# Keeping converted weights in a DRAM scratch: an attention and squared-ReLU MLP kernel on one core

## The chip, the core and the metric

The kernel runs on one core of a Trainium2 chip. The core has TensorE (PE; its weight loads are shown as PEld), VectorE (DVE), ScalarE (ACT), GpSimd (POOL) and SyncE (SP), which here only issues DMAs. Times are microseconds on the device for one execution.

## What is computed

q, k and v have the shape (4, 12, 448, 64): four batches, twelve heads. The weights are arrays of 64-bit floats, w_in 768 x 2048 and w_out 2048 x 768. The output is 1792 x 768 in 32-bit floats.

```python
scores = scale * np.matmul(q, k.transpose(0, 1, 3, 2))
scores = np.where(mask, -1000000000.0, scores)      # causal
attn = softmax(scores)
x = (attn @ v), heads side by side                  # 1792 x 768
h = np.maximum(x @ w_in, 0.0)
out = (h * h @ w_out).astype(np.float32)
```

## The kernel before

The tokens are worked in two halves of 896 (two batches each). The heads go in pairs: twelve pairs of the first half, then twelve of the second, whose results are stored to a DRAM tensor `x_dram` (line 435) and loaded back later (line 591). A pair takes scores on PE (line 327), the row maximum on DVE (line 340), the exponential on ACT (line 344), a scaling on POOL (line 353), transposes on PE (line 367) and the product with v (line 387).

The MLP runs in four groups of 512 of the 2048 inner columns, once for each half. A group has a first product, x by w_in (lines 490 to 492, `h_unit`), and a second one, the squares by w_out (lines 526 to 528, `o_unit`). Each number is kept as two parts, a high one rounded to PE's input format and a low one that holds the rest, and three matmuls make one product: high by high, high by low, low by high. Tiles with a 2 in front of their columns (`x`, `wi`, `g`, `wo`) hold both parts.

The weights come as 64-bit words. `piece` (line 441) brings one block: for w_in 128 x 512 (six blocks a group, tile `wi`), for w_out 128 x 384 (eight a group, tile `wo`). It loads the raw words (line 467, three buffers), has ACT make two intermediate words, has DVE shift, add and combine them into a 32-bit float (lines 475, 243 and 478), and splits that into the two parts (lines 250 and 247 on POOL, or line 240 on ACT and 243 on DVE). Each half does this for all 56 blocks.

The order of all instructions comes from a planner (class `Plan`). Every step gives an engine or a choice of engines with a duration, what it reads and writes, and a rank; the planner takes at each turn the step that can start first by its own clock, and the rank decides between equals. The emitted order of each engine is that of the planned starts. Nearly all DMAs are issued by SP in that order: q, k and v loads (lines 290 and 302), raw weights, x tiles and outputs. An issue that has to wait holds up all that stand behind it on SP. Buffers of the odd pairs (`b...`) are given up after the twelfth pair, and `wo` lies in their place (`swap`). In the first group of the first half, the first product is done for the first six pairs while later pairs are still in work.

Of the kernel before, what the change touches and what calls it, by code (L numbers as in the profile page):

```python
# [8 lines left out]
F32 = mybir.dt.float32  # L9
# [7 lines left out]
PE, ACT, DVE, POOL, DMA, DMA2 = range(6)  # L17
# [131 lines left out]
def kernel(  # L149
# [17 lines left out]
    nc = tc.nc  # L167
# [3 lines left out]
    P = 128  # L171
# [3 lines left out]
    NP = H // 2  # L175
# [3 lines left out]
    GF = 4  # L179
    NG = DFF // P // GF  # L180
    CH = DM // 2
# [23 lines left out]
    plan = Plan()  # L205
# [7 lines left out]
    wi_t = const.tile([P, 2, NP, GF * P], F32R, name="wi")  # L213
# [16 lines left out]
    for i in range(2):  # L230
        m = mask[i * QC:(i + 1) * QC, S - QC:]
        nc.gpsimd.affine_select(
            out=m, in_=m, pattern=[[-1, QC]], base=0,
# [203 lines left out]


    late = {"wo": None, "acc": None}

    def piece(rank, kind, gr, a, ch, after):
        if kind == "i":
# [121 lines left out]
    swap = [plan.op(0.0, [(DMA, 0.0, enter)], after=list(plan.ops))]  # L564

    def group(ph, gr, rank, step, begin):

        for c in range(NP):
            piece(begin + (rank - begin) * (c + 0.5) / NP, "i", gr, c, 0, ())
        begin = rank  # L570
        if ph == 0 and gr == 0:
            r = NP * PAIR + 16
            for f in range(GF):
                r = h_unit(f, 0, r, (start - r) / (GF - f) / NP)
            for f in range(GF):
                rank = h_unit(f, 1, rank, H_US * step)
        else:
            for f in range(GF):
                for h in range(2):
                    rank = h_unit(f, h, rank, H_US * step)  # L580
        for i in range(2 * GF):
            piece(begin + (rank - begin) * (i + 0.5) / 8, "o", gr, i % GF, i // GF, swap)
        begin = rank
        for ch in range(2):
            for t in range(NT):
                rank = o_unit(ph, gr, t, ch, rank, O_US * step, swap)
        return begin, rank
# [8 lines left out]
    rank, begin = start, 10.0  # L596
    rest = NG * (2 * GF * NP * H_US + 2 * NT * GF * O_US) - GF * NP * H_US
    for gr in range(NG):
        begin, rank = group(0, gr, rank, (rest + NA * 7.0) / rest, begin)
# [4 lines left out]
    for ph in range(1, NPH):  # L604
        for gr in range(NG):
            begin, rank = group(ph, gr, rank, 1.0, begin)
# [33 lines left out]
```

## Time and profile before

| | |
|---|---|
| timed runs | 642.58, 639.98, 642.56 us; median 642.56 |
| the profiled execution, first to last instruction | 638.4 us (no other time is given for it) |
| PE, PEld, DVE busy | 97%, 85%, 71% |
| ACT, POOL busy | 56%, 62% |
| DMA | 78.61 MB, mean 123 GB/s |
| HBM read, written | 69.60 MB, 8.26 MB |

Busy shares are of the span. The profile also has a row of the clock granted to TensorE by slices, the groups of instructions by source line with what ended the idle time before them, the waits, and the chain of waits: the work that ended last, followed back. In names, buffer numbers are left out: `raw<-in_moe_w_in_dram` is a load into any of the three raw buffers.

### The profile page before, as it was taken

The numbers are of one execution on the slowest core, as the hardware profiler recorded it, in microseconds if no ns is written. First come the engines' busy times: TensorE is split into PE (matmuls) and PEld (weight loads), VectorE is DVE, ScalarE is ACT, GpSimd is POOL, SyncE is SP. The second block draws the span as 40 slices with busy tenths as digits, with TensorE's granted clock in tenths as the row PEclk, the third lists the DMA queues.
The fourth block names the chain that finished last, engine by engine and source line by source line (L and its number), as shares of the span: only waits on it lengthen the run. The fifth ranks groups of instructions, "written<-read, shape, count | busy, mean of one in ns | idle before, by whom it ended". The sixth has DMA issues, their size and how long they took to land.

```text
span 638.4 us, 11482 instructions
## 1 busy us (share of the span) xinstructions
PE 619.2 (97%) x3936; PEld 544.8 (85%) x3936; DVE 450.4 (71%) x911; ACT 356.7 (56%) x856; POOL 395.8 (62%) x498
## 2 busy tenths in 40 slices
PE   3999999999999999999999999999999999999997
PEld 2666777798888898789888889999999999999997
DVE  5789865686668787678885479759845993897022
ACT  4789977676787456675557553545653344333300
POOL 1567854775678655767576688876657556656410
PEclk9799999999999999999999999999999999999999
DMA  9898931545574546544463258723541453141022
GB/s 156 158 201 150 186 80 31 109 154 152 118 173 130 151 98 155 152 96 115 126 159 100 77 164 248 210 73 109 158 130 34 108 155 101 59 123 50 1 87 87
DMA packets 134779, 78.61 MB, mean 123 GB/s; under 512 B 113729, under 2 KB 120385, under 8 KB 134721
## 3 DMA queue, kind: packets, MB, share of 16 engines
q1 hardware_dynamic: 131008, 77.42, 47.2%
q10 hardware_dynamic: 3712, 0.46, 0.5%
q8 instruction: 31, 0.51, 0.3%
q14 instruction: 28, 0.22, 0.1%
HBM read 69.60 MB, written 8.26 MB: 122 GB/s over the span
## 4 chain that ended last, share of the span: by engine, by line
PE 84%; DVE 5%; DMA 3%; POOL 3%; ACT 2%; issue 1%; SPq 0%; DVEq 0%; POOLq 0%; ACTq 0%
PE ps L526 12%; PE ps L527 12%; PE ps L528 12%; PE ps L490 11%; PE ps L491 11%; PE ps L492 11%; PE ps L387 6%; PE ps L367 5%; PE ps L327 4%; POOL ap L353 3%; DVE ps L340 2%; DMA v<-in_v_dram 1%; DMA bq<-in_q_dram 1%; ACT ap L344 1%; DMA aq<-in_q_dram 1%
## 5 line engine op out<-in xcount | busy, mean ns | idle before, releaser
L526 PE MATMUL ps<-wo,g 128*128 128x384 f32 x448 | 153.2, 342 | 0.0
L527 PE MATMUL ps<-wo,g 128*128 128x384 f32 x448 | 151.2, 338 | 0.0
L528 PE MATMUL ps<-wo,g 128*128 128x384 f32 x448 | 151.2, 337 | 0.0
L490 PE MATMUL ps<-x,wi 128*128 128x448 f32 x384 | 145.0, 378 | 0.6 <-ACT x L240 0.6
L491 PE MATMUL ps<-x,wi 128*128 128x448 f32 x384 | 140.6, 366 | 0.2 <-DVE x L243 0.2
L492 PE MATMUL ps<-x,wi 128*128 128x448 f32 x384 | 140.5, 366 | 0.0
L240 ACT ACTIVATE b<-raw 128x384 int32<-128x384 uint32 (+1 forms) x112 | 68.3, 610 | 89.1 <-DVE z L243 80.3
L243 DVE CUSTOM_DVE_ANT_0 z<-z,b 128x768 uint16<-128x768 uint16 (+1 forms) x112 | 102.9, 919 | 8.8 <-ACT b L240 1.9
L478 DVE SCALAR_TENSOR_TENSOR z<-raw,z 128x384 int32<-128x384 int32 (+1 forms) x112 | 94.8, 846 | 2.9
L353 POOL TENSOR_SCALAR ap<-ap,asm 128x448 f32<-128x448 f32 (+6 forms) x123 | 71.5, 600 | 35.1 <-DVE asm L411 21.8
L340 DVE CUSTOM_DVE_ANT_0 ps<-ps,mask 128x448 f32<-128x448 f32 (+6 forms) x168 | 68.8, 443 | 33.9 <-PE ps L327 24.9
L240 ACT ACTIVATE z<-raw 128x384 f32<-128x384 f32 (+1 forms) x112 | 67.8, 609 | 32.6 <-POOL wi L247 15.6
L526 PEld LDWEIGHTS ps<-wo,g 128*128 128x128 f32 x448 | 84.2, 188 | 1.4 <-issue 1.0
L527 PEld LDWEIGHTS ps<-wo,g 128*128 128x128 f32 x448 | 84.2, 188 | 0.1
L528 PEld LDWEIGHTS ps<-wo,g 128*128 128x128 f32 x448 | 84.1, 188 | 0.0
L490 PEld LDWEIGHTS ps<-x,wi 128*128 128x128 f32 x384 | 72.2, 188 | 9.0 <-issue 1.7
L475 DVE TENSOR_SCALAR z<-z 128x384 int32<-128x384 int32 (+1 forms) x112 | 63.3, 565 | 23.3 <-ACT z L240 23.0
L243 DVE TENSOR_TENSOR acc<-ps,acc 128x384 f32<-128x384 f32 x84 | 46.0, 550 | 46.1 <-PE ps L528 45.8
L492 PEld LDWEIGHTS ps<-x,wi 128*128 128x128 f32 x384 | 72.1, 188 | 6.1
L491 PEld LDWEIGHTS ps<-x,wi 128*128 128x128 f32 x384 | 72.2, 188 | 5.8 <-DVE x L243 0.5
L344 ACT ACTIVATE ap<-ps,mx 128x448 f32<-128x448 f32 (+6 forms) x126 | 58.7, 481 | 14.3 <-DVE mx L340 13.9
L247 POOL TENSOR_TENSOR g<-r,g 128x448 fp32r<-128x448 f32 x52 | 64.9, 1249 | 2.4
(65 smaller groups left out, 848.3 us busy)
## 6 DMA issues: line engine op xcount, KB each, us to landing
raw<-in_moe_w_in_dram SPq DMA_DIRECT2D x48, 512.0 KB, 3.9
raw<-in_moe_w_out_dram SPq DMA_DIRECT2D x64, 384.0 KB, 3.4
out_dram<-acc SPq DMA_DIRECT2D x28, 192.0 KB, 2.5
v<-in_v_dram SPq DMA_DIRECT2D x24, 192.0 KB, 4.0
ak<-in_k_dram SPq DMA_DIRECT2D x72, 56.0 KB, 2.7
aq<-in_q_dram SPq DMA_DIRECT2D x68, 56.0 KB, 2.6
x_dram<-xs SPq DMA_DIRECT2D x12, 224.0 KB, 3.8
xs<-x_dram SPq DMA_DIRECT2D x12, 224.0 KB, 2.7
```

The source lines that it names most:

```text
L240: return (ACT, t_act(n, psum, more), lambda: nc.scalar.activation(dst(), src(), func, **kw))
L243: return (DVE, t_dve(n) + more, lambda: nc.vector.tensor_tensor(out=dst(), in0=a(), in1=b(), op=op))
L340: plan.op(at, [(DVE, t_dve(w), lambda: nc.vector.tensor_tensor_reduce(out=at_(), in0=at_(), in1=mask[:, S - w:], scale=-SCALE, scalar=3.0e ...
L344: plan.op(at, [(ACT, t_act(w, True, 0.5), lambda: nc.scalar.activation(probabilities(c), at_(), AF.Exp, bias=mx.t, scale=-1.0, accum_out=s ...
L353: (POOL, 0.0005 * CW[c] + 0.34, lambda: nc.gpsimd.tensor_scalar(*operands(), 1.0, op0=ALU.mult, op1=ALU.mult)),
L478: plan.op(rank - 2, [(DVE, t_dve(n) + 0.2, lambda: nc.vector.scalar_tensor_tensor(out=z(), in0=word(1), scalar=-2 ** 31, in1=z(), op0=ALU. ...
L490: nc.tensor.matmul(o, w[:, 0], x[:, 0], start=c == 0, stop=False)
L491: nc.tensor.matmul(o, w[:, 0], x[:, 1], start=False, stop=False)
L492: nc.tensor.matmul(o, w[:, 1], x[:, 0], start=False, stop=c == NP - 1)
L526: nc.tensor.matmul(res(), g[:, 0], w[:, 0], start=f == 0, stop=False)
L527: nc.tensor.matmul(res(), g[:, 0], w[:, 1], start=False, stop=False)
L528: nc.tensor.matmul(res(), g[:, 1], w[:, 0], start=False, stop=f == GF - 1)
```

## The change

The scratch `w_dram` has a place for the two parts of every block, as 32-bit floats: 128 x 2 x 512 for w_in, 128 x 2 x 384 for w_out, 8 bytes a weight as in the raw form. In the first half (`ph == 0`) each block is converted as before and then stored from `wi` or `wo` into its place (`keep`, rank + 2). In the second half nothing is converted: `fetch` loads both parts straight into `wi` or `wo`. There is no buffer between, so a `fetch` is ordered behind the matmuls that read the old block. Each counts 1.7 us of the planner's DMA queue.

```diff
--- before.py
+++ after.py
@@ -437,6 +437,28 @@
 
 
     late = {"wo": None, "acc": None}
+    w_dram = {
+        "i": nc.dram_tensor("wi_split", (NG, NP, P, 2, GF * P), F32, kind="Internal").ap(),
+        "o": nc.dram_tensor("wo_split", (NG, 2 * GF, P, 2, CH), F32, kind="Internal").ap(),
+    }
+
+    def dst_of(kind, a, ch):
+        t = wi_t[:, :, a] if kind == "i" else late["wo"][:, :, a, ch * CH:(ch + 1) * CH]
+        return t.bitcast(F32)
+
+    def place_of(kind, gr, a, ch):
+        i = a if kind == "i" else a + GF * ch
+        return w_dram[kind][gr, i], ("wd", kind, gr, i), ("wi", a) if kind == "i" else ("wo", a, ch)
+
+    def keep(rank, kind, gr, a, ch):
+        place, saved, key = place_of(kind, gr, a, ch)
+        plan.op(rank, [(DMA, 1.7, lambda: nc.sync.dma_start(out=place, in_=dst_of(kind, a, ch)))],
+                [(key, 0), (key, 1)], [saved])
+
+    def fetch(rank, kind, gr, a, ch):
+        place, saved, key = place_of(kind, gr, a, ch)
+        plan.op(rank, [(DMA, 1.7, lambda: nc.sync.dma_start(out=dst_of(kind, a, ch), in_=place))],
+                [saved], [(key, 0), (key, 1)])
 
     def piece(rank, kind, gr, a, ch, after):
         if kind == "i":
@@ -565,8 +587,15 @@
 
     def group(ph, gr, rank, step, begin):
 
+        def weights(rank, *which):
+            if ph == 0:
+                piece(rank, *which, swap if which[0] == "o" else ())
+                keep(rank + 2, *which)
+            else:
+                fetch(rank, *which)
+
         for c in range(NP):
-            piece(begin + (rank - begin) * (c + 0.5) / NP, "i", gr, c, 0, ())
+            weights(begin + (rank - begin) * (c + 0.5) / NP, "i", gr, c, 0)
         begin = rank
         if ph == 0 and gr == 0:
             r = NP * PAIR + 16
@@ -579,7 +608,7 @@
                 for h in range(2):
                     rank = h_unit(f, h, rank, H_US * step)
         for i in range(2 * GF):
-            piece(begin + (rank - begin) * (i + 0.5) / 8, "o", gr, i % GF, i // GF, swap)
+            weights(begin + (rank - begin) * (i + 0.5) / 8, "o", gr, i % GF, i // GF)
         begin = rank
         for ch in range(2):
             for t in range(NT):
```

The queue of SP among the early heads, around the fifth to seventh pair: `ak` and `bk` are k loads of an odd and an even pair (the first pair is an `a`), `aq` and `bq` their q loads, `raw_80` to `raw_82` the three raw buffers, `v_90` one of two v buffers. Before:

```order
L467 DMA raw_81<-in_moe_w_in_dram 128x512
L290 DMA bk<-in_k_dram 32x14x32 x4
L290 DMA bq<-in_q_dram 32x14x32 x4
L290 DMA ak<-in_k_dram 32x14x32 x4
L290 DMA aq<-in_q_dram 32x14x32 x4
L467 DMA raw_82<-in_moe_w_in_dram 128x512
L467 DMA raw_80<-in_moe_w_in_dram 128x512
L467 DMA raw_81<-in_moe_w_in_dram 128x512
L302 DMA v_90<-in_v_dram 128x6x64 x3
L302 DMA v_90<-in_v_dram 64x6x64
```

Below is the same place in the changed kernel, where `wi_split` is the scratch for w_in:

```order
L489 DMA raw_81<-in_moe_w_in_dram 128x512
L290 DMA bk<-in_k_dram 32x14x32 x2
L455 DMA wi_split<-wi 256x1x512
L290 DMA bk<-in_k_dram 32x14x32 x2
L290 DMA bq<-in_q_dram 32x14x32 x4
L290 DMA ak<-in_k_dram 32x14x32 x4
L290 DMA aq<-in_q_dram 32x14x32 x4
L489 DMA raw_82<-in_moe_w_in_dram 128x512
L489 DMA raw_80<-in_moe_w_in_dram 128x512
L302 DMA v_90<-in_v_dram 128x6x64 x3
L302 DMA v_90<-in_v_dram 64x6x64
L455 DMA wi_split<-wi 256x1x512
```

A store stands between the second and third k load of the sixth pair, another behind the v loads, and one of the three raw loads ahead of the v loads has gone further back.

PE, around the eighth pair of heads (`b...` are its tiles, `a...` those of the pairs beside it): line 367 transposes, 327 scores, 387 the product with v, and 490 to 492 (after: 512 to 514) the first product, where `x_68` is the sixth tile of x, which goes with the sixth block of w_in. Before:

```order
L490 MATMUL ps_108<-x_68,wi 128x448
L491 MATMUL ps_108<-x_68,wi 128x448
L492 MATMUL ps_108<-x_68,wi 128x448
L490 MATMUL ps_105<-x_68,wi 128x448
L491 MATMUL ps_105<-x_68,wi 128x448
L492 MATMUL ps_105<-x_68,wi 128x448
L367 MATMUL ps_103<-ident,bp 128x128 x4
L490 MATMUL ps_104<-x_63,wi 128x448
L491 MATMUL ps_104<-x_63,wi 128x448
L492 MATMUL ps_104<-x_63,wi 128x448
L490 MATMUL ps_104<-x_64,wi 128x448
L491 MATMUL ps_104<-x_64,wi 128x448
```

In the changed kernel the first rows of PE with `x_68` have these around them:

```order
L387 MATMUL ps_109<-bpt,v_90 64x64 x2
L367 MATMUL ps_103<-ident,ap 128x128 x4
L367 MATMUL ps_104<-ident,ap 128x128 x4
L367 MATMUL ps_107<-ident,ap 128x128 x4
L367 MATMUL ps_103<-ident,ap 128x128 x4
L512 MATMUL ps_108<-x_68,wi 128x448
L513 MATMUL ps_108<-x_68,wi 128x448
L514 MATMUL ps_108<-x_68,wi 128x448
L512 MATMUL ps_105<-x_68,wi 128x448
L513 MATMUL ps_105<-x_68,wi 128x448
L514 MATMUL ps_105<-x_68,wi 128x448
L512 MATMUL ps_109<-x_63,wi 128x448
```

The matmuls with `x_68` stood ahead of the transposes of the eighth pair; now they stand behind that pair's whole work and the next pair's transposes.

SP around the start of the second half: `acc` is the output tile of the first half, `wo_split` the scratch for w_out. Before:

```order
L467 DMA raw_82<-in_moe_w_out_dram 128x384
L544 DMA out_dram<-acc 128x384 x2
L467 DMA raw_80<-in_moe_w_out_dram 128x384
L544 DMA out_dram<-acc 128x384
L467 DMA raw_81<-in_moe_w_in_dram 128x512
```

In the changed kernel the last outputs of the first half are followed by these:

```order
L566 DMA out_dram<-acc 128x384
L460 DMA wo<-wo_split 128x2x384
L566 DMA out_dram<-acc 128x384
L460 DMA wo<-wo_split 128x2x384 x2
L460 DMA wi<-wi_split 128x2x512 x6
L460 DMA wo<-wo_split 128x2x384 x8
```

Where raw loads stood, the loads of both parts stand in blocks of six and eight in the order of use.

## Rows read from the trace of the kernel before

**Rows 1.** The page: busy us, share and instructions of each engine.
```profile
PE 619.2 (97%) x3936; PEld 544.8 (85%) x3936; DVE 450.4 (71%) x911; ACT 356.7 (56%) x856; POOL 395.8 (62%) x498
```

**Rows 2.** Windows of 40 us: length, busy us of PE, PEld, DVE, ACT, POOL, clock, DMA, GB/s.
```profile
0.00:20.00 20.00, 9.51 (x68) 5.54 (x69) 11.94 (x48) 9.87 (x33) 5.51 (x18) 0.86 0.91 156
...
340.00:380.00 40.00, 38.95 (x242) 33.32 (x241) 22.18 (x41) 22.45 (x53) 30.43 (x36) 1.00 0.35 106
380.00:420.00 40.00, 40.00 (x213) 38.53 (x212) 35.01 (x48) 19.69 (x36) 30.28 (x32) 1.00 0.71 206
...
620.00:638.40 18.40, 14.84 (x86) 14.51 (x84) 4.46 (x8) 0.00 (x0) 0.00 (x0) 1.00 0.26 91
```

**Rows 3.** Windows by stage: the early heads, the rest of the first half, the second half.
```profile
30.00:78.60 48.60, 46.49 (x407) 31.33 (x407) 43.25 (x139) 44.14 (x134) 35.12 (x57) 1.00 0.91 182
...
120.00:399.60 279.60, 277.43 (x1804) 244.88 (x1805) 214.03 (x431) 173.04 (x414) 192.76 (x225) 1.00 0.52 139
399.60:634.00 234.40, 234.40 (x1247) 225.25 (x1247) 150.42 (x193) 91.84 (x168) 133.38 (x149) 1.00 0.33 99
```

**Rows 4.** Timeline of PE around and after the start of the second half (start us, us, instruction).
```profile
394.82 0.34 PE L528 MATMUL ps<-wo,g 128*128 128x384 f32 x1
...
399.59 0.34 PE L528 MATMUL ps<-wo,g 128*128 128x384 f32 x1
...
399.97 0.37 PE L491 MATMUL ps<-x,wi 128*128 128x448 f32 x1
...
413.55 0.36 PE L492 MATMUL ps<-x,wi 128*128 128x448 f32 x1
...
434.50 0.34 PE L528 MATMUL ps<-wo,g 128*128 128x384 f32 x1
...
439.69 0.34 PE L528 MATMUL ps<-wo,g 128*128 128x384 f32 x1
...
469.43 0.37 PE L491 MATMUL ps<-x,wi 128*128 128x448 f32 x1
...
471.91 0.37 PE L491 MATMUL ps<-x,wi 128*128 128x448 f32 x1
```

**Rows 5.** The chain of waits in the first 70 us (start us, us, what).
```profile
40.76 5.21 DMA v<-in_v_dram
...
54.97 0.48 SPq L290
...
57.06 2.10 DMA bq<-in_q_dram
```

**Rows 6.** Timeline of SP's DMA issues among the early heads.
```profile
27.66 1.94 SPq L290 DMA_DIRECT2D bk<-in_k_dram  x4
...
38.08 5.91 SPq L302 DMA_DIRECT2D v<-in_v_dram  x4
```

**Rows 7.** Groups by line from 400 us on, conversion on DVE: busy us, mean ns, idle.
```profile
L243 DVE CUSTOM_DVE_ANT_0 z<-z,b 128x768 uint16<-128x768 uint16 (+1 forms) x46 | 49.9, 1085 | 2.9
...
L478 DVE SCALAR_TENSOR_TENSOR z<-raw,z 128x384 int32<-128x384 int32 (+1 forms) x46 | 38.1, 828 | 1.3
...
L475 DVE TENSOR_SCALAR z<-z 128x384 int32<-128x384 int32 (+1 forms) x46 | 27.2, 591 | 7.5 <-ACT z L240 7.3
```

**Rows 8.** DMA issues of the page: count, KB each, median us to landing.
```profile
raw<-in_moe_w_in_dram SPq DMA_DIRECT2D x48, 512.0 KB, 3.9
...
x_dram<-xs SPq DMA_DIRECT2D x12, 224.0 KB, 3.8
xs<-x_dram SPq DMA_DIRECT2D x12, 224.0 KB, 2.7
```

**Rows 9.** Timeline of POOL, the second half of the split of w_in blocks.
```profile
24.30 1.27 POOL L247 TENSOR_TENSOR wi<-z,wi 128x512 fp32r<-128x512 f32 x1
...
37.64 1.28 POOL L247 TENSOR_TENSOR wi<-z,wi 128x512 fp32r<-128x512 f32 x1
...
67.94 1.29 POOL L247 TENSOR_TENSOR wi<-z,wi 128x512 fp32r<-128x512 f32 x1
```

## The prediction

> **What bounds the kernel now.** I read the page first, then the table by windows, then the chain of waits of the first 70 us, the issues of the SP queue there, and last the timeline of TensorE in the second half.
>
> The page says that PE is busy 619.2 of 638.4 us [rows 1]. The table by windows says where the other 19.2 us lie: 20.00 - 9.51 = 10.5 us in the first 20 us, before the first scores are there, and 18.40 - 14.84 = 3.6 us at the end, for the last addition and the last store [rows 2]. That leaves 19.2 - 10.5 - 3.6 = 5.1 us over the 600 us between, of which 40.00 - 38.95 = 1.05 us lie in the stretch from 340 to 380 us [rows 2].
>
> The second half of the tokens runs from 399.6 us. PE is busy 234.40 of 234.40 us there [rows 3], so no wait of PE can be taken away from it. That the pace is that of the matmuls themselves shows in their starts: 27 of 384 columns, just ahead of it, start in 399.59 - 394.82 = 4.77 us, 176.7 ns each, and 67 of 448 columns in 413.55 - 399.97 = 13.58 us, 202.7 ns each [rows 4]. A group's first product (x by w_in) has 8 x 6 x 3 = 144 of the long matmuls and its second product (squares by w_out) 14 x 4 x 3 = 168 of the short: 29.2 + 29.7 = 58.9 us; four groups are 235.5 us, which is the length of the half. DVE, with 150.42 us, and POOL, with 133.38 us, are far from full beside it [rows 3].
>
> Only the early stretch looks different. From 30 to 78.6 us DVE is busy 43.25 and ACT 44.14 of 48.60 us and the DMA engines 91% [rows 3]. The chain of waits leaves PE there: it runs through the landing of a v load (5.21 us), then through single issues of the SP queue (0.48 us each) and the landing of a q load (2.10 us) [rows 5]. SP is slow to issue there: four k loads take it 1.94 us, four v loads with their wait 5.91 us [rows 6].
>
> **What is removed.** In the second half 56 blocks of weights (4 groups of 6 of w_in and 8 of w_out) are no longer converted: per block two ACT, three DVE and two splitting instructions, 392 in all. The largest of their groups after 400 us is 49.9 us of DVE [rows 7]. All of it lies beside a PE that never waits, so I book 0 us. The loads into the raw buffer go too, and a load of the same number of bytes comes in their place (8 bytes a weight in either form).
>
> **Does the reading back cost anything?** A load into wi must wait for the last matmul that reads the old block, at the end of the group's first product; from there the second product covers it for 168 x 0.1767 = 29.7 us. Six loads of 524,288 bytes are 3.15 MB. From 380 to 420 us the engines moved 206 GB/s at a busy share of 0.71 [rows 2], so 206 / 0.71 = 290 GB/s when full: 1.81 us a load, 10.8 us for six, and 3.9 us of landing [rows 8]. 14.7 us lie inside 29.7 us with half to spare. The eight loads of wo have the same bytes and the 29.2 us of the next first product; four of them can start half a product sooner. In SP's order they stand as six, eight, six, eight, in the order in which they are wanted, with nothing late in front of them. Half of the cover would have to go before a load came late; without any, it would be 14.7 us at each of the seven borders between products of this half. I book 0 us.
>
> The pace of PE itself is not fixed, and this bounds the half from both sides. In some products the spacing is lower: 30 short matmuls in 439.69 - 434.50 = 5.19 us, 173.0 ns, and in some higher: 12 long ones in 471.91 - 469.43 = 2.48 us, 206.7 ns [rows 4]. I see no engine whose work goes with it: it changes at the borders of products, while the conversions go on. By the starts in the same timeline one first product of this half ran slow (144 x 4.0 ns = 0.58 us) and two second ones (168 x 3.7 ns = 0.62 us each). All quick would be -1.8 us, all slow (three more long ones, two more short ones) +3.0 us. I take 0, the level of before.
>
> **What is added in the first half.** 56 stores, 25.7 MB, each issued by SP after the block's split, which SP must wait for; behind it stand raw loads and q, k and v loads. After 120 us the DMA engines are 52% busy [rows 3], and the 50 or so stores that fall there are 50 x 1.81 = 91 us at most of 280: 85%, which fits. Nor do the waits for splits hold up the conversions: in the new order the raw load of a block stands behind the store of a block four or five before it, and it has to wait anyway until the block three before it has left the raw buffer, which is later.
>
> Before 80 us it does not simply fit. Up to the q loads of the twelfth pair of heads the new order has four stores more and two w_out loads less. The first store stands in the middle of the four k loads that SP issues from 27.66 us [rows 6]; the split that it waits for started at 24.30 us and took 1.27 [rows 9], so it does not wait. The next split ends at 37.64 + 1.28 = 38.9 us [rows 9], and the second store's place is behind the v loads that start at 38.08 and take SP 5.91 us [rows 6]. So the price is not waiting but room. Two more issues at 0.48 us are 1.0 us of a queue that never pauses. Four stores of 1.81 less two loads of 393,216 bytes (1.36 each) are 7.2 - 2.7 = 4.5 us of all DMA engines, and 9% of 48.6, 4.4 us, are free in the stretch: they just fit, if the free time comes where it is wanted. From below the price is 0 (the loads are asked for ahead of need), from above 1.0 + 7.2 = 8.2 us, if each store holds up the loads behind it by its whole length. The trace has no store of this size; the nearest are the x stores, 224 KB in 3.8 us, where a load of the same tile takes 2.7 [rows 8]. I take the two issues, and the 1.1 us by which a store lands later than a load once, for the store that parts the four k loads: +2.1 us.
>
> The Trainium skill (Perfetto Trace Analysis, section Identifying the Most-Contended Engine) says that the busy share of matmuls is not a good measure of how near TensorE is to its limit, and that the busy share of the weight loads is a better one. From 30 to 78.6 us these are 46.49 against 31.33 of 48.60 us [rows 3]. By the first, PE is full but for 2.1 us and the sum below stands; by the second 17.3 us are open, the stretch is as long as its loads make it, and the time is that of the first rival below. The chain, which leaves PE in this stretch, sides with the page.
>
> **What is moved.** The raw loads of the fifth and sixth blocks of w_in come later in SP's order, behind the stores. So the matmuls with the sixth block stand later on PE: before the tenth pair's scores there are 30 matmuls of the first product instead of 45, before the eleventh's 42 instead of 60. In the old trace the sixth block's split ended at 67.94 + 1.29 = 69.2 us [rows 9], and these products filled PE between the pairs. 15 x 0.203 = 3.0 us of filling are taken out of the busiest stretch. That costs 3.0 us if the pairs come no sooner, and nothing if they do, for with two conversions fewer in the stretch, 1.09 + 0.83 + 0.59 = 2.5 us of DVE each [rows 7], the engine gets 5.0 us back. I take +1.0 us.
>
> From 340 to 380 us, before the change of halves, the first conversions for the second half disappear from POOL and DVE; PE idles 1.05 us there [rows 2]. I take -1.0 us; 0 if the last heads' chain alone makes it.
>
> **The sum.** 2.1 + 1.0 - 1.0 + 0 = +2.1 us on the profiled 638.4 us: 640.5 us. No other time of that execution is given; the timed runs are 639.98 to 642.58 us, so the span lies 4.2 us under their median. I put the difference on the median: 642.56 + 2.1 = 644.7 us. By its own bounds (the pace -1.8 to +3.0, the moved matmuls 0 to +3.0, the stretch before the half -1.0 to 0) the forecast reaches from 642.56 - 1.8 - 1.0 = 639.8 to 642.56 + 2.1 + 3.0 + 3.0 = 650.7 us.
>
> **Rivals.** *The loads of the early heads become the bound (slower).* Four stores go down the same queue ahead of k, q and v loads that are wanted next, in the stretch where SP never pauses and the engines are 91% busy. If nothing hides them they cost the 8.2 us of the upper bound, and the 3.0 us of moved matmuls are lost beside it: 642.56 + 11.2 = 653.8 us. It decides as soon as a load behind a store lands after PE has used up what stands ahead of it. For it speaks the chain [rows 5]; against it that PE still is busy 46.49 of 48.60 us there [rows 3].
>
> *Less work beside PE makes it quicker (faster).* All products of the second half at the lower spacing, -1.8 us; the idle time before the half gone, -1.05; two conversions fewer among the early heads, -5.0 us of DVE on a chain that leaves PE: 642.56 - 7.9 = 634.7 us. Against it: the lower spacing stands beside busy engines too, and DMA is as full as DVE in the early stretch.
>
> *The weights come late (the change does not hold its cover).* If the read-backs wait behind other transfers for a whole landing, 3.9 us at each of seven borders: 27 us, 670 us. Only at the first border do outputs and x loads stand between them.
>
> **Chances.** Forecast 0.58, early loads 0.27, less work beside PE 0.12, late weights 0.03. A measurement of this kernel can tell about 0.5%, 3.2 us, from no change: 639.3 to 645.8 us. Faster takes 0.09 of the faster rival and 0.02 of the forecast's lower end: 0.11. Slower takes 0.25 of the early loads, 0.03 of the late weights and 0.08 of the forecast's upper end: 0.36. The same: 0.53. The range from 638 to 653.8 us leaves out the larger part of the faster rival, the late weights and what lies beyond the early loads' full price, about 0.2.
>
> **What would show it.** In the new trace DVE, ACT and POOL have no conversions after 400 us, and PE still shows no idle time and takes 58.9 us a group. If the second half is shorter by more than 2 us, the pace depends on the work beside it and I am wrong there. If PE waits for a wi or wo load in it, the cover is wrong. The first half should be 1 to 3 us longer, with the loss before 100 us, SP's issues solid, and q or k landings longer than 2.7 us. If the loss lies after 120 us, the waits of the stores for their splits are what I undervalued; if the first half is shorter, the early heads were held by DVE.

## The result and the profile after

The changed kernel takes 645.55 us (median of 4 runs, 645.17 to 645.94), the kernel before beside it 641.27 us (639.76 to 642.58): ratio 1.0072, 95% interval 1.0048 to 1.0095. That is +4.3 us by the medians and +4.6 us by the ratio. The profiled spans say +4.9: 643.3 against 638.4 us.

First the page, then the stretches of [rows 3] in the new trace (the second half now runs from 403.3 us):

```profile
PE 619.5 (96%) x3936; PEld 545.5 (85%) x3936; DVE 296.5 (46%) x731; ACT 294.1 (46%) x744; POOL 297.5 (46%) x398
```

```profile
30.00:78.60 48.60, 40.11 (x357) 26.72 (x354) 35.54 (x118) 35.86 (x109) 26.23 (x48) 0.93 0.83 179
120.00:399.60 279.60, 279.55 (x1829) 247.72 (x1828) 190.09 (x406) 164.19 (x405) 183.01 (x222) 1.00 0.72 216
403.30:639.00 235.70, 235.70 (x1248) 225.98 (x1248) 23.42 (x42) 42.84 (x78) 55.14 (x64) 1.00 0.29 100
```

and the 40 us before the change of halves, as in [rows 2]:

```profile
340.00:380.00 40.00, 40.00 (x267) 34.05 (x266) 14.35 (x43) 21.78 (x56) 24.32 (x33) 1.00 0.34 105
```

PE's busy time is what it was [rows 1]; DVE has lost 154 us and ACT 63. In the second half PE still never waits, and DVE fell from 150.42 to 23.42 us [rows 3] without any gain. Among the early heads PE is busy 40.11 instead of 46.49 of 48.60 us. From 120 us to the last matmul it waits for 0.05 us in all; before it was 2.2 [rows 3].

These are windows by what was lost and what came back, of the kernel before and then of the changed one (length, busy PE, PEld, DVE, ACT, POOL, clock, DMA share, GB/s):

```profile
20.00:100.00 80.00, 77.89 (x673) 53.71 (x672) 64.45 (x211) 67.04 (x202) 53.07 (x88) 0.97 0.75 150
100.00:380.00 280.00, 277.00 (x1840) 240.17 (x1839) 204.69 (x434) 179.63 (x440) 188.28 (x230) 1.00 0.48 125
```

```profile
20.00:100.00 80.00, 69.89 (x605) 47.13 (x607) 60.17 (x197) 63.19 (x191) 42.75 (x76) 0.95 0.82 181
100.00:380.00 280.00, 279.95 (x1885) 242.91 (x1878) 194.40 (x433) 177.15 (x443) 184.92 (x230) 1.00 0.68 199
```

PE loses 8.0 us from 20 to 100 us and gets 2.95 back from 100 to 380: 5.0 us. That this is just the difference of the spans is in part chance: by its first matmul (at 399.76 and 403.31 us) the second half starts 3.5 us later, and from its first to its last matmul it takes 1.1 us more (235.85 against 234.74) without any wait, by the slower of the two spacings [rows 4]. Two executions of the kernel before differ by about 1 us in each of the two stretches (idle 2.1 and 3.0 us in this one, 3.2 and 2.2 in another), so no single window is good to better than that.

Where PE stands in the early stretch shows the chain of waits of the changed kernel, which now leaves PE for the raw weights:

```profile
36.78 5.03 DMA raw<-in_moe_w_in_dram
...
60.59 5.96 DMA raw<-in_moe_w_in_dram
...
69.96 6.17 DMA raw<-in_moe_w_in_dram
```

In the chain before there were a v load, single issues of SP and a q load at this place [rows 5]. The waits of ACT for raw blocks of w_in from 20 to 110 us (in all, times, longest), of the kernel before and then of the changed one:

```profile
ACT z L240 <- DMA raw<-in_moe_w_in_dram: 1.3, 1, 1.3
```

```profile
ACT z L240 <- DMA raw<-in_moe_w_in_dram: 10.2, 3, 5.5
```

The timeline of ACT (in brackets the idle time ahead and what ended it), and then PE's at the same moment, show how a weight load can hold up the heads:

```profile
59.55 1.58 ACT L240 ACTIVATE bpt<-ps 128x512 f32<-128x512 f32 x3
66.63 0.66 ACT L240 ACTIVATE z<-raw 128x512 f32<-128x512 f32 x1 [5.49 <-DMA raw<-in_moe_w_in_dram]
67.19 0.65 ACT L240 ACTIVATE b<-raw 128x512 int32<-128x512 uint32 x1
67.74 0.63 ACT L344 ACTIVATE bp<-ps,mx 128x448 f32<-128x448 f32 x1
```

```profile
68.51 1.97 PE L367 MATMUL ps<-ident,ap 128*128 128x128 f32 x8 [4.37 <-ACT bp L344]
```

ACT works in order. At its head stands the conversion of the fifth block of w_in, whose raw load SP issued only at 60.59 us; ACT does nothing for 5.49 us, the exponentials of the next pair wait behind the conversion, and PE waits 4.37 us for them. PE stood still from 64.1 us on, and from 66 to 72 us the granted clock is 0.50, the lower of its two levels (1.2 GHz); the mean from 60 to 100 us is 0.91 where it had been 1.00. The 8 transposes of the row take 1.97 us; 10 of them had taken 1.32 us ten us earlier.

The page's DMA issues:

```profile
raw<-in_moe_w_in_dram SPq DMA_DIRECT2D x24, 512.0 KB, 4.4
wi_split<-wi SPq DMA_DIRECT2D x24, 512.0 KB, 4.1
...
wi<-wi_split SPq DMA_DIRECT2D x24, 512.0 KB, 6.5
```

A store of 512 KB lands as quickly as a raw load of that size (4.1 and 4.4 us in this run); the nearest row I had was the x store that took 1.1 us longer than the load [rows 8].

### The profile page after: what moved, and what is told of

Its sections match the earlier page's. It is cut to its first block, busy times and chain, and to the rows that moved or that the text cites. A ratio compares the mean times of both kernels' runs of the same rounds, so it can differ in the third digit from the quotient of the medians.

```text
span 643.3 us, 11116 instructions
## 1 busy us (share of the span) xinstructions
PE 619.5 (96%) x3936; PEld 545.5 (85%) x3936; DVE 296.5 (46%) x731; ACT 294.1 (46%) x744; POOL 297.5 (46%) x398
## 4 chain that ended last, share of the span: by engine, by line
PE 87%; DMA 5%; DVE 3%; ACT 2%; POOL 2%; issue 1%; SPq 1%; ACTq 0%; DVEq 0%; POOLq 0%
PE ps L548 13%; PE ps L512 12%; PE ps L549 12%; PE ps L550 12%; PE ps L513 12%; PE ps L514 12%; PE ps L367 5%; PE ps L387 5%; PE ps L327 4%; DMA raw<-in_moe_w_in_dram 3%; DVE ps L340 1%; ACT bp L344 1%; POOL ap L353 1%; DMA bq<-in_q_dram 1%; DMA aq<-in_q_dram 1%
## 5 line engine op out<-in xcount | busy, mean ns | idle before, releaser
L240 ACT ACTIVATE r<-ps 128x448 f32<-128x448 f32 x64 | 34.9, 547 | 168.4 <-PE ps L514 167.8
L250 POOL TENSOR_SCALAR g<-r 128x448 fp32r<-128x448 f32 x50 | 29.3, 586 | 166.5 <-ACT r L240 166.1
L353 POOL TENSOR_SCALAR ap<-ap,asm 128x448 f32<-128x448 f32 (+6 forms) x117 | 66.2, 588 | 37.7 <-DVE asm L411 18.9
L247 POOL TENSOR_TENSOR g<-r,g 128x448 fp32r<-128x448 f32 x56 | 67.5, 1205 | 3.4
L367 PE MATMUL ps<-ident,ap 128*128 128x128 f32 x288 | 43.7, 291 | 9.5 <-ACT bp L344 4.4
L500 DVE SCALAR_TENSOR_TENSOR z<-raw,z 128x384 int32<-128x384 int32 (+1 forms) x56 | 48.5, 866 | 1.5
L367 PEld LDWEIGHTS ps<-ident,ap 128*128 128x128 f32 x288 | 35.3, 147 | 15.9 <-POOL ap L353 7.6
```

The costliest lines, as they stand in the source:

```text
L247: lambda: nc.gpsimd.tensor_tensor(out=dst(), in0=a(), in1=b(), op=op))
L353: (POOL, 0.0005 * CW[c] + 0.34, lambda: nc.gpsimd.tensor_scalar(*operands(), 1.0, op0=ALU.mult, op1=ALU.mult)),
L367: nc.tensor.transpose(ps.t[:, n * P:(n + 1) * P], s.p[:, POFF[c] + kc * P:POFF[c] + (kc + 1) * P], ident[:, o:o + P])
L500: plan.op(rank - 2, [(DVE, t_dve(n) + 0.2, lambda: nc.vector.scalar_tensor_tensor(out=z(), in0=word(1), scalar=-2 ** 31, in1=z(), op0=ALU. ...
```

## The experiments

Two theories. *Order*: the raw loads of the fifth and sixth blocks stand later in SP's order (behind stores that the planner books at 1.7 us), and ACT stands at them. *Bytes*: the early stores themselves, 512 KB each, hold up what comes behind them. A third matter was what the removed conversions are worth. The table gathers all runs. Idle times of PE (length of the window minus busy PE) and ACT's waits for raw weights of either kind (20 to 110 us) are read as above from the profiled execution of each. A time with a plus or a minus in the text is the ratio's share of 641 us.

| kernel | ratio to before, 95% | PE idle 20-100 | 100-380 | ACT's waits |
|---|---|---|---|---|
| before (two executions) | 1 | 2.1, 3.2 | 3.0, 2.2 | 1.3, 4.6 |
| changed | 1.0072 (1.0048 to 1.0095) | 10.1 | 0.05 | 10.2 |
| e1 stores held | 1.0002 (0.9988 to 1.0016) | 4.1 | 2.7 | 4.6 |
| e2 small stores | 1.0012 (1.0000 to 1.0024) | 5.9 | 0.3 | 6.9 |
| e3 stores only | 1.0075 (1.0057 to 1.0094) | 8.5 | 1.5 | 9.3 |
| e5 stores booked cheap | 1.0032 (1.0019 to 1.0046) | 7.2 | 1.2 | 3.1 |
| e6 six stores, old order | 1.0064 (1.0042 to 1.0085) | 6.3 | 2.5 | 6.6 |
| e7 no weights in second half | 0.9972 (0.9960 to 0.9984) | 3.7 | 1.6 | 4.4 |
| e8 held and cheap | 0.9989 (0.9973 to 1.0005) | 4.9 | 1.6 | 4.2 |
| e9 conversions later | 1.0036 (1.0020 to 1.0053) | 5.2 | 1.3 | 0.8 |
| e10 before, conversions later | 1.0043 (1.0017 to 1.0068) | 6.4 | 2.4 | 7.2 |
| e11 held, cheap, later | 1.0148 (1.0121 to 1.0174) | 5.3 | 4.5 | 6.1 |
| e12 six small stores, old order | 1.0012 (0.9993 to 1.0031) | 2.8 | 2.7 | 3.3 |

**e1, stores held.** The six stores of the first group of w_in wait until all twelve pairs are done.

```diff
-                [(key, 0), (key, 1)], [saved])
+                [(key, 0), (key, 1)], [saved], after=swap if kind == "i" and gr == 0 else ())
```

> The six stores of the first group's w_in blocks wait until the twelve pairs of the first half are done; nothing else of the change is altered. Theory A (the planner moves the raw loads of the fifth and sixth w_in blocks back behind the stores, and ACT, which takes its work in order, stands at those conversions with the exponentials behind it): the two loads are back at their old place, ACT no longer waits 7.5 us for them, PE is busy 38 of 40 us from 20 to 60 us and 39.8 of 40 from 60 to 100, and the time is 645.6 - 7.4 = 638.1 us, below the kernel before, since the 3.0 us won after 100 us stay. Rival B (the stores take room on the DMA engines, wherever they stand): six stores at once cost again between 115 and 150 us, and the time stays at 643 us or more. Rival C (what was won after 100 us came from the early order): 641.3 us, as before.

640.87 us against 640.92: neither 638.1 nor 643, but as rival C had it. The raw loads of the fifth and sixth blocks are back in their old places too. So the loss hangs on the early place of these six stores, by order or by bytes, and not on the other 50 nor on the reading back.

**e2, small stores.** Same order as the changed kernel, but the stores and read-backs of the first group of w_in move 8 of 512 columns.

```diff
+    def part(t, kind, gr):
+        return t[:, :, :8] if kind == "i" and gr == 0 else t
...
-        plan.op(rank, [(DMA, 1.7, lambda: nc.sync.dma_start(out=place, in_=dst_of(kind, a, ch)))],
+        plan.op(rank, [(DMA, 1.7, lambda: nc.sync.dma_start(
+            out=part(place, kind, gr), in_=part(dst_of(kind, a, ch), kind, gr)))],
...
```

(`fetch` in the same way; the second half's first group then works with what else lies in `wi`.)

> The order of every engine is that of the changed kernel, with all its waits; only the six stores of the first group's w_in blocks (and their read-backs) move 8 of 512 columns, so the second half's first group works with weights that are not the right ones. Theory A: the order makes the loss, so it stays: the fifth w_in load is still issued at about 60 us, it lands perhaps 1 us sooner than the 6.0 us of the changed kernel, ACT still waits 4 to 5 us for it, PE is busy about 34 of 40 us from 60 to 100, and the time is 643.5 to 645.5 us. Rival B: the bytes make the loss: PE is busy 39 or more of 40 us there and the time is about 638.5 us.

641.89 us, +0.8, between what the two theories had asked for: without the bytes nearly all of the loss is gone, though the order is the new one. Yet PE idles 5.9 us in the early stretch, and the scores of the fourteenth pair (the same work stands ahead of them) start at 136.45 us; in the kernel before at 132.2, in the changed one at 139.7. I first read this as 4.2 us for the order and 3.3 for the bytes. But the order gives back what it takes, since PE then idles 0.3 us from 100 to 380 us, so a split at that pair is no split of the time. The stop shown above is here too: the same conversion waits 4.74 us on ACT (5.49 in the changed kernel) and PE 3.27 us for the exponentials behind it (4.37). Most of that one stop thus comes with the order; full stores add 1.1 us to it, and 2.4 us to PE's waits for ACT's copies `bpt` (from 20 to 110 us 2.7 us instead of 0.3).

**e3, stores only.** Converted in both halves, stored, never read back.

```diff
-            if ph == 0:
-                piece(rank, *which, swap if which[0] == "o" else ())
+            piece(rank, *which, swap if which[0] == "o" else ())
+            if ph == 0:
                 keep(rank + 2, *which)
-            else:
-                fetch(rank, *which)
```

> Half of the change alone: the first half converts and stores as in the changed kernel, the second half converts again from the raw weights and nothing is read back. Theory A: the early loss of 7.4 us is there in full, as the early order is the same. What was won after 100 us tells its source: if it came from the conversions that no longer run beside the last heads, it is gone and the time is 641.3 + 7.4 = 648.7 us; if it came from another order of the first half, it stays and the time is about 645.6 us. Rival B gives 648 us or more too, with PE's loss also in the stretch after 120 us, where the DMA engines then carry raw loads and stores.

645.25 us: the whole loss with the second half's conversions back in place. PE idles 1.17 us from 340 to 380 us again (changed kernel: 0), but the time does not show it: the ratios of e3 and of the changed kernel differ by 0.03%, far inside their intervals.

**e4, the kernel before again**, for one more trace; it gave the second figures in the table, and the last section has what it says of the pace.

> The kernel before, unchanged, profiled once more, for the pace of the matmuls: in its first profile three of the eight products of the second half ran at 206.7 or 176.7 ns a matmul (the second group's first product, the second and third groups' second ones) and five at 202.7 or 173.3. If the pace belongs to the program (addresses, places of instructions), the same three are slow. If it belongs to the execution, others are, and the 1 to 3 us between runs of one kernel come from it; time 639.8 to 642.6 us.

**e5, stores booked cheap.** The planner counts 0.5 us for a store. The raw loads of the fifth and sixth blocks then go out together at 49.82 us, ahead of the 60.59 and 69.96 us of the changed kernel. The sixth is so about where the kernel before has it (48.44 us), but the fifth is not: there it is the last of the three from 36.53 us on.

```diff
-        plan.op(rank, [(DMA, 1.7, lambda: nc.sync.dma_start(out=place, in_=dst_of(kind, a, ch)))],
+        plan.op(rank, [(DMA, 0.5, lambda: nc.sync.dma_start(out=place, in_=dst_of(kind, a, ch)))],
```

> One number differs from the changed kernel: the planner books a store with 0.5 us instead of 1.7. All stores and read-backs stay, with all their bytes, and the stores stay early; but in SP's order the raw loads of the fifth and sixth w_in blocks go back to where they stood before the change, and the counts of first-product matmuls ahead of each pair are those of the kernel before. Order theory (late raw loads at the head of ACT's queue are the cause): most of the early loss goes, TensorE busy 85 us or more of the first 100 us, ACT's wait for raw w_in between 20 and 110 us under 4 us, time 640.5 to 642.5 us. Bytes theory (the early stores hold the loads up on the DMA engines): the loss stays, busy 80 to 82 us of the first 100, time 644 us or more. If both shares of 4.2 and 3.3 us add up as the small and the full stores suggested: 644.5 - 4.2 = about 641 to 642 us, with a loss of about 3 us before the fourteenth pair.

642.52 us, +2.0: between the two theories, and a test of neither alone, as one raw load is still late. ACT's waits for weights are down to 3.1 us, but PE still idles 7.2 us early.

**e6, six stores in the old order.** The kernel before, with the first group's stores alone, booked at nothing.

```diff
-        plan.op(rank, [(DMA, 1.7, lambda: nc.sync.dma_start(out=place, in_=dst_of(kind, a, ch)))],
+        plan.op(rank, [(DMA, 0.0, lambda: nc.sync.dma_start(out=place, in_=dst_of(kind, a, ch)))],
...
+            piece(rank, *which, swap if which[0] == "o" else ())
+            if ph == 0 and gr == 0 and which[0] == "i":
+                keep(rank + 2, *which)
...
```

> The kernel before, and only the six stores of the first group's w_in blocks added, booked at nothing by the planner, so that the order of everything else is that of the kernel before; nothing is read back and the second half converts again. It measures the early bytes and SP issues alone, in the old order. Bytes theory: +3 us, 644 us, TensorE busy about 84 us of the first 100. Order theory: 0 to +1 us, 641 to 642 us, busy 86 to 87 us, ACT's waits for raw w_in below 4 us.

645.21 us, +4.1 (2.7 to 5.4 by the interval): almost the whole loss without the new order. The order theory fell here.

**e12, six small stores in the old order.** e6 with 8 of 512 columns to a store.

```diff
-        plan.op(rank, [(DMA, 0.0, lambda: nc.sync.dma_start(out=place, in_=dst_of(kind, a, ch)))],
+        plan.op(rank, [(DMA, 0.0, lambda: nc.sync.dma_start(
+            out=place[:, :, :8], in_=dst_of(kind, a, ch)[:, :, :8]))],
```

> The run with six stores in the old order again (no read-back, the second half converts), but each store moves 8 of its 512 columns: the same six issues of SP at the same places, almost no bytes. Bytes theory (the stores' transfers hold up the loads behind them until ACT stands at a weight load): time back to 640.5 to 641.5 us, ACT's waits for raw weights 20 to 110 us under 4 us, TensorE idle 20 to 100 us 2 to 4 us. Issue theory (it is SP's time, some 0.55 us a store, and its waits for the splits): the 4.1 us stay, 644 us or more, ACT's waits above 6 us.

641.73 us, +0.8. With e2, e6 and the changed kernel this makes a square: small stores cost 0.12% in either order, full ones 0.64% in the old and 0.72% in the new. The bytes are 0.52 and 0.60%, 3.3 and 3.8 us. The six issues alone are +0.8 us in the old order (-0.4 to +2.0 by the interval). What the new order costs by itself is not separated: e2 and the changed kernel also leave out the second half's conversions, whose gain (e7 below: 1.0 to 2.6 us) lies in their times, and e3, which converts, lies 0.11% above e6 with overlapping intervals and 50 stores more.

How the bytes act shows the timeline of SP (a row of several issues goes from the start of the first to the end of the last). The changed kernel behind its first four stores:

```profile
27.73 0.57 SPq L455 DMA_DIRECT2D wi_split<-wi  x1
...
29.00 1.01 SPq L290 DMA_DIRECT2D bk<-in_k_dram  x1
...
43.24 0.58 SPq L455 DMA_DIRECT2D wi_split<-wi  x1
43.91 2.71 SPq L290 DMA_DIRECT2D bk<-in_k_dram  x4
...
54.50 0.55 SPq L455 DMA_DIRECT2D wi_split<-wi  x1
55.15 2.63 SPq L290 DMA_DIRECT2D bk<-in_k_dram  x4
...
59.97 0.52 SPq L455 DMA_DIRECT2D wi_split<-wi  x1
60.59 0.55 SPq L489 DMA_DIRECT2D raw<-in_moe_w_in_dram  x1
61.23 2.50 SPq L290 DMA_DIRECT2D ak<-in_k_dram  x4
```

And e2, the same order with small stores:

```profile
28.15 0.57 SPq L458 DMA_DIRECT2D wi_split<-wi  x1
...
29.41 0.48 SPq L290 DMA_DIRECT2D bk<-in_k_dram  x1
...
44.08 2.12 SPq L290 DMA_DIRECT2D bk<-in_k_dram  x4
...
53.99 2.31 SPq L290 DMA_DIRECT2D bk<-in_k_dram  x4
...
59.11 0.55 SPq L494 DMA_DIRECT2D raw<-in_moe_w_in_dram  x1
59.75 1.95 SPq L290 DMA_DIRECT2D ak<-in_k_dram  x4
```

The issue of the store takes the same time with few bytes or with many (0.57 us). What differs is the loads behind it: the second k load takes SP 1.01 us instead of 0.48, and each set of four 0.32 to 0.59 us more: 0.53 + 0.59 + 0.32 + 0.55 = 2.0 us behind four stores. 1.4 us of these lie ahead of the raw load of the fifth block. It goes out 1.48 us later than in e2, though SP reached the first store 0.42 us earlier: 1.9 us. SP also waits for others, for some 10 us between 20 and 70 us, and these waits did not take the delay up; they added 0.5 us to it. The next raw load is 69.96 - 67.59 = 2.4 us late. The old order shows the same: behind its first four stores the rows of k loads are 0.48, 0.52, 0.55 and 0.85 us longer in e6 than in e12, the first three of them ahead of the first w_out load, which goes out at 63.08 instead of 60.62 us. Why an issue behind a full store takes longer, the traces don't say. The load of the fifth block also lands slower with full stores, in 5.96 us against 5.41 in e2; how much of the 3.3 to 3.8 us goes through the issues and how much through the landings is not separated.

**e7, no weights in the second half.** The bound on the gain.

```diff
-            piece(begin + (rank - begin) * (c + 0.5) / NP, "i", gr, c, 0, ())
+            if ph == 0:
+                piece(begin + (rank - begin) * (c + 0.5) / NP, "i", gr, c, 0, ())
```

(and the same for w_out)

> The kernel before, without any raw load or conversion of weights in the second half (it leaves out: the second half multiplies by whatever weights the first half left). No scratch, no store. It shows the most that removing the second conversion can give. By my account only the 1.05 us of idle time from 340 to 380 us: 639.5 to 640.5 us against 641, TensorE 40.00 of 40 us in every window of the second half as before, its length 234.5 to 236. If work beside TensorE set its pace (my rival of the prediction), the second half would be 1.8 us shorter and the time below 638.5.

639.02 us against 640.68: -1.8 us by the ratio (-2.6 to -1.0). The second half has its old length, 234.7 us from its first to its last matmul. Only the stretch ahead of it gained: the half starts at 398.46 us instead of 399.76, the 1.05 us that I had booked and a few tenths more. By its interval, leaving out the second conversion is worth no more than 0.4% in this order of the rest.

**e8, held and cheap**: e1 and e5 together.

```diff
-        plan.op(rank, [(DMA, 1.7, lambda: nc.sync.dma_start(out=place, in_=dst_of(kind, a, ch)))],
-                [(key, 0), (key, 1)], [saved])
+        plan.op(rank, [(DMA, 0.5, lambda: nc.sync.dma_start(out=place, in_=dst_of(kind, a, ch)))],
+                [(key, 0), (key, 1)], [saved], after=swap if kind == "i" and gr == 0 else ())
```

> The changed kernel with the first group's six w_in stores held back until the twelve pairs are done, and all stores booked at 0.5 us instead of 1.7. If holding the stores takes away the early loss, and the cheaper booking also leaves the raw loads of the later blocks where they were, it has the old early heads and the 1 us of the stretch before the second half: 639.5 to 640.5 us, at best 0.2% under the kernel before. If the gain of 2.4 us after 100 us goes with the early stores' order rather than with anything that was removed, it comes out as the held stores did: 640.9 us.

640.56 against 640.68: the best version of the scratch, and not to be told from the kernel before.

**e9 and e10, later conversions.** The planner takes a raw load of the first group to land 4 us later, so ACT's conversions stand further back in its order; e9 is the changed kernel, e10 the kernel before. SP's order changed with it: in e9 the raw loads of the fifth and sixth blocks go out at 54.39 and 61.15 us, ahead of the 60.59 and 69.96 us of the changed kernel.

```diff
-                t.ready = max(t.ready, end + (0.0 if same else self.LAG[e]))
+                t.ready = max(t.ready, end + (0.0 if same else self.LAG[e]) + o.late)
...
+        o.late = 4.0 if gr == 0 else 0.0
```

> The changed kernel, but the planner is told that a raw load of the first group of the first half lands 4 us later than it assumed. ACT's conversions then stand behind more of the exponentials in ACT's order, and SP asks for the raw loads at about the same places; every store and read-back stays, early, with all its bytes. Queue theory (the loss comes because ACT works strictly in order and stands at a weight load that has not landed, with the exponentials of the next pair behind it): ACT's wait for raw w_in between 20 and 110 us falls from 10.2 to under 3 us, TensorE's loss before the fourteenth pair from 7.5 to under 3 us, time 641 to 642.5 us. Room theory (the early stores take the time of SP and of the DMA engines themselves, and something else waits instead, q, k or v loads): ACT's wait falls, but the loss stays at 5 us or more, time 644 us or more.

> The control for the run beside it: the kernel before with the same 4 us in the planner and no scratch, store or read-back. If the later conversions are worth nothing without stores, 640.5 to 641.5 us, and what the changed kernel gains by them is the stores' loss given back. If they take first-product matmuls out of the early stretch, up to 1 % of it: 642 us. If the kernel before lost by the same queue, 639.5 us.

e9: 643.06 us, +2.3, half of the loss; ACT's wait for raw w_in is 0.8 us instead of 10.2. So part of the price goes through ACT's queue, but as the loads also come earlier, e9 does not tell whether the stores' part or the order's. And e10, with no store at all, is 2.8 us slower than before, more than any of the three expectations had, and the timelines of its ACT and PE show the same stop as the changed kernel, at a load of w_out:

```profile
72.70 0.54 ACT L241 ACTIVATE b<-raw 128x384 int32<-128x384 uint32 x1 [5.04 <-DMA raw<-in_moe_w_out_dram]
```

```profile
74.00 0.63 PE L368 MATMUL ps<-ident,bp 128*128 128x128 f32 x4 [3.19 <-ACT ap L345]
```

In the stops shown here, what holds up the early heads is a weight load that is late for its place in ACT's order, whatever made it late. Between e9 and e10 the whole scratch makes no difference (their intervals overlap), but the 4 us move other work too, so how much of the 4.3 us goes through ACT is not settled.

**e11, all remedies** (e8 with the 4 us), meant to beat both kernels.

> The changed kernel with the six stores of the first group held until the twelve pairs are done, stores booked at 0.5 us, and the 4 us of the planner for raw loads of the first group: both remedies together, as the version meant to beat both kernels. If they add to the 1.7 us that leaving out the second half's weights was worth: 639 us, 0.2 to 0.3% under the kernel before. If the held stores give all back in the stretch after 100 us: 640.5 us, no difference to tell.

650.21 us, the slowest of all. Its profiled execution was its quickest, 646.09 us; there PE idles 4.5 us from 100 to 380 us, where the others have 0.05 to 3.0, and ACT waits 5.5 us for a w_out load. Its slower runs had a mean granted clock of 0.984 to 0.989, the profiled one 0.992; what made them slower, and with it most of the 9.5 us, is not explained.

## Why the prediction was right and where it was not

The time lies in the range, 0.9 us over the number. That it comes so near is partly luck: I counted from a median of 642.56 us, and with a fourth run that median is 641.27. The change itself is +4.3 to +4.6 us, more than twice the +2.1 of the sum. The place was right, the early stretch of the first half, and so was the kind, early stores that make later loads late; the size was not, and neither was what waits for them: raw w_in loads through ACT. By the prediction's bound of 0.5% the outcome is slower, which I gave 0.36, against 0.53 for no difference. It lies between the forecast, +2.1, and the rival of the early loads, +11.2.

- *Second half, removed work, 0 us*: right. PE 235.70 of 235.70 us, and e7 shows the same length without any conversion.
- *Read-back, 0 us*: right. A load of wi lands in 6.5 us and not in the 3.9 that I took from the raw loads [rows 8], and the cover of 29.7 us takes it.
- *340 to 380 us, -1.0*: right in the trace. The idle 1.05 us [rows 2] are gone and come back in e3, whose time does not tell them; e7 gives 1.8 us in the runs.
- *Waits of stores for splits, 0*: right; between 0 and 130 us SP waits 1.2 us in all for wo and 1.1 for wi.
- *Room, +2.1*: the step that was mis-sized. I counted net, "two more issues" and one load that lands 1.1 us later. The six early stores alone, without the moved loads, measured +4.1 us (e6). It is the stores one by one that count: four of them before 64 us, each 0.55 us of SP for its issue and some 0.5 us for the loads behind it. e2 against the changed kernel makes the bytes 0.0060 x 641 = 3.8 us, e6 against e12 3.3. I had argued that 4.5 us of the DMA engines' time would fit into 4.4 us that were free. The mean share did not tell the price: SP's issues lie on the chain there [rows 5], and they got longer. Whether full DMA engines make them longer is open. Nor was SP "a queue that never pauses": from 20 to 70 us it waited for others for some 11 us in the kernel before and 10 in the changed one, and the delay came through all the same.
- *Moved matmuls, +1.0*: the place was right, with the cause one step earlier. The raw loads that were moved back stop ACT, and ACT stops PE; I had only seen the matmuls that fill. The order with small stores is +0.8 us (e2), and that holds the six issues and the gain of the second half too, so this term has no measurement of its own.

The 0.8 us of e2 and the 3.8 us of the bytes make up the 4.6 us by the way they are taken, which proves nothing more. The point at which the rival was to decide, a load behind a store that lands after PE has used up what stands ahead, is what happened, with less than half of its price and with weights in place of k, q and v; why not the whole price is not shown. Of the signs that I had named, the loss before 100 us came, the first half is 3.5 us longer and not 1 to 3, and the landings are unclear: between 25 and 75 us the k loads of the even pairs take 4.3 us (3.9 before), those of the odd ones 2.3 (3.1 before).

*Less work beside PE makes it quicker* is refuted for the second half: with DVE at 23 instead of 150 us it is not shorter, in e7 neither. Of that rival's price only the 1.05 us of idle time came. *Late weights* did not occur.

The rule of the Trainium skill that the prediction weighed (Perfetto Trace Analysis, section Identifying the Most-Contended Engine) points the right way for this stretch: from 30 to 78.6 us the weight loads were busy 31.33 us where the matmuls showed 46.49 [rows 3], and the stretch did lengthen with its loads. The price that the prediction hung on it, +11.2 us, was further from the +4.6 than the sum's +2.1. The Trainium skill (DMA: Bandwidth & Descriptors, section Issuing engines are not separate DMA queues) calls the time that a sequencer takes to start a DMA usually small beside the DMA. For a single k load this trace agrees: 0.48 us against 2.3 to 4.3 to its landing. It does not hold for a set of them, whose landings overlap while the issues follow one another: four k loads took SP 2.1 us, and 2.7 behind a store.

## What to carry to other kernels

Work that is taken off an engine is worth only what the path's engine waited for it: 1.05 us of idle PE in the trace before was about this gain (1.0 to 2.6 us in e7), and the price came from where the new transfers were put. In a stretch where the chain of waits runs through one queue's issues, count each new DMA with its issue and with what it does to the issues behind it, not only the free bytes; and look at what stands at the head of each in-order engine when a load gets later. Test order and bytes apart, with transfers made small at the same place, and judge by the whole time, since a milestone inside can show a loss that is given back.

## What had not been expected of the hardware

An issue on SP behind a store of 512 KB takes up to 1.01 us, against 0.48 behind one of 8 KB at the same place. Behind a raw load of the same 512 KB it does not: in the kernel before, the four k loads after the raw load of 48.44 us took 1.94 us.

The two spacings of the matmuls [rows 4] belong to the execution, not to the program. These are starts in the first second product of the second half, of the kernel before and then of the same program run again:

```profile
429.47 0.33 PE L526 MATMUL ps<-wo,g 128*128 128x384 f32 x1
...
456.51 0.33 PE L526 MATMUL ps<-wo,g 128*128 128x384 f32 x1
```

```profile
427.83 0.34 PE L526 MATMUL ps<-wo,g 128*128 128x384 f32 x1
...
456.45 0.34 PE L526 MATMUL ps<-wo,g 128*128 128x384 f32 x1
```

156 matmuls in 27.04 us are 173.3 ns each, 162 in 28.62 us are 176.7, at a granted clock of 1.00 both times. The spacing changes at borders between products and differs from one execution to the next. It is worth 0.6 us a product and so, by estimate, a part of the scatter of the runs; its cause is open.
